# Loading the queries and keys of two attention units together, and moving the second unit's scores ahead of the first unit's PV

## The chip, the cores and the metric

The kernel runs on one core of a Trainium2 chip. The time is in device microseconds (us), measured around the whole execution on the chip. Before the change, 8 runs gave a median of 291.63 us, from 290.91 to 292.34. One further look at the kernel is an execution that was recorded by the hardware profiler.

## What is computed

The inputs q, k and v have the shape 8 x 8 x 576 x 64 (batch, heads, tokens, head dimension), in float32. Attention runs in chunks of 64 tokens; each chunk attends to itself alone. The result goes through two matrix products with a gated activation between them. The reference, cut to its core:

```
q_c = q.reshape(B, H, nc, 64, D)              # the same for k and v; nc = 9
scores = q_c @ k_c.transpose / sqrt(D)
attn = exp(scores - max); attn = attn / sum(attn)
x = (attn @ v_c)  ->  [B*S, H*D]              # 4608 tokens x 512
h = x @ w_in                                  # 512 x 2048
g = h * (1 / (1 + exp(-beta * h)))            # beta has one value per column of h
out = g @ w_out                               # 2048 x 512, float32 result
```

The kernel works in float16 with float32 accumulation. It leaves out the maximum in the softmax (the scores are small) and writes the gate as h * (tanh(beta * h / 2) + 1) / 2.

## The kernel before

**Units and blocks.** The 4608 tokens are cut into 18 units of 256 tokens for the attention, and two units make a block of 512 tokens for the two products. For each unit the kernel goes through these steps:

1. Load q, k (`load_qk`, L102) and two tiles of v (`load_v`, L110) from the GpSimd queue (POOL), converting to float16 on the way. For units 0 to 7, a partition holds two neighbouring tokens.
2. Transpose q and k in blocks of 32x32 on the vector engine (DVE), in `emit_T` (L154).
3. Multiply the scores on TensorE (PE), `emit_sc` (L231), into a PSUM tile of two banks with the tag "s", and take Exp on the scalar engine (ACT), L240.
4. Multiply by v, `emit_pv` (L256), once for each of the two 128-token tiles of the unit, the first into a PSUM tile "x", the second into "s". A column of ones in v gives the sum of the row.
5. Divide by that sum on DVE, `emit_norm`: a reciprocal (L267) and one or two multiplications (L271).
6. Transpose the result, on PE for the first units (`emit_xt_pe`, L287, into PSUM, followed by ACT's copy to the tile xt, L288), later by a DMA.

For each block, `emit_m` makes one 128-row slice m of h (four matmuls, L303, into a PSUM tile "p"), tanh on ACT (L313) and the multiply-add on DVE (L317) into gt; there are 16 slices. `emit_t` makes the second product for one tile of 128 tokens (L335), and ACT copies it out (L345).

**PSUM.** The pool "p" has four buffers of one bank, which are given out in turn; "s" and "x" have one buffer of two banks each. [...]

**The order of the work** is written out by hand: each engine executes its instructions in the order of the calls. The start of the kernel is special:

- Unit 0 is loaded in two halves of four heads. The first half of q and k comes through the queue of the sync engine (SP) as float32 into `raw0`, and is converted on ACT (L173) and DVE (L176). The second half comes through POOL with the conversion (L360). `emit_T_half` transposes a half (L177), `emit_sc_half` multiplies it (L194) and takes Exp (L202). Only after that do PV, norm and the transposes of unit 0 follow.
- Unit 1 is loaded whole by `load_qk(1)`, and its scores come after unit 0 has been transposed.
- The first six slices of block 0 are made in halves: columns 0:256 (unit 0) first, columns 256:512 (unit 1) when unit 1 is done.
- `emit_idle` (L352) multiplies zeros into an unused "p" buffer between these steps. It holds a place in the PE order and keeps the array working.

The order of POOL's loads at the start is: second half of unit 0's q and k; v tiles 0 and 1; q and k of unit 1; w_in group 0; v tiles 2 and 3; the identity for the transposes; w_in groups 1 to 7; w_out groups 0 to 2; unit 2; w_out group 3; unit 3 and later units. Each w_in group holds two slices m.

Of the kernel before, what the change touches and what calls it, by code (L numbers as in the profile page):

```python
# [15 lines left out]
def kernel(  # L16
# [41 lines left out]
    raw0 = [const.tile([128, HH, 2, D], FP32, name=f"raw{i}") for i in range(2)]  # L58
    qk0 = [[const.tile([128, HH, 2, D], FP16, name=f"h0{i}{a}") for i in range(2)] for a in range(2)]
    qkT0 = [[const.tile([128, HH, CH, 2], FP16, name=f"t0{i}{a}") for i in range(2)] for a in range(2)]  # L60
# [81 lines left out]
    def emit_T(u, which=("kT", "qT")):  # L142
# [17 lines left out]
        if "qT" in which and u not in (6, 7, 8):  # L160
            loads_to(u + 4)
# [9 lines left out]
    def emit_T_half(a):  # L171
        if a == 0:
            nc.scalar.copy(out=qk0[a][0], in_=raw0[0])  # L173
        for i in (0, 1):
            if a == 0 and i == 1:
# [3 lines left out]
                    "p (h i r) -> p h r i", h=HH, r=2),  # L179
                in_=qk0[a][i].rearrange("p h r d -> p (h r d)").bitcast(FP32).rearrange(  # L180
                    "p (h r i) -> p h r i", h=HH, r=2),
            )

    def emit_sc_half(a):
        if a == 0:
            et_t[0] = et_p.tile([128, 2, H, CH], FP16, tag="et", name="et")
            x_t["s0"] = ps_s.tile([128, 2, H, CH], FP32, tag="s", name="sc")
        sc = x_t["s0"]
        qt, kt = qkT0[a]
        for h in range(HH):  # L190
            for e in range(2):
                for c in range(4):
                    p0, o0 = 32 * c, 64 * (c % 2)
                    nc.tensor.matmul(  # L194
                        out=sc[o0:o0 + 64, c // 2, HH * a + h, :],
                        lhsT=kt[p0:p0 + 32, h, :, e],
                        rhs=qt[p0:p0 + 32, h, :, e],
                        start=(e == 0),
                        stop=(e == 1),
                    )  # L200
        hs = slice(HH * a, HH * a + HH)
        nc.scalar.activation(out=et_t[0][:, :, hs], in_=sc[:, :, hs], func=ACTF.Exp, scale=scale)  # L202
# [44 lines left out]
    def emit_pv(u):  # L247
        et = et_t.pop(u)
        for s in range(2):
            i = 2 * u + s  # L250
            pool, tag = ((ps_x, "x"), (ps_s, "s"))[s]
            x = pool.tile([128, 2, 4, 128], FP32, tag=tag, name="x")
            for g in range(4):
                for r in range(2):
                    for c in range(2):
                        nc.tensor.matmul(  # L256
                            out=x[64 * c:64 * c + 64, r, g, 0:D + 1],
# [6 lines left out]
    def emit_norm(u, s):  # L264
        x = x_t.pop((u, s))
        rd = rd_p.tile([128, 2, 4, 1], FP32, tag="rd", name="rd")
        nc.vector.reciprocal(out=rd, in_=x[:, :, :, D:D + 1])  # L267
        x16 = x_p.tile([128, 2, 4, D], FP16, tag="x16", name="x16")
        for r in ([0, 1] if u < 2 else [slice(0, 2)]):
            o = x16[:, r]  # L270
            nc.vector.tensor_tensor(  # L271
                out=o, in0=x[:, r, :, 0:D], in1=rd[:, r].to_broadcast(list(o.shape)), op=ALU.mult
            )
# [8 lines left out]
    def emit_xt_pe(u, s):  # L282
        xf = x16_t.pop((u, s)).rearrange("p r h d -> p (r h d)")
        pool, tag = (ps_x, "x") if s == 0 else (ps_s, "s") if u == 2 else (ps_p, "p")
# [69 lines left out]
    with tc.manual_schedule():  # L354
# [3 lines left out]
        for a, eng, dst in ((0, nc.sync, raw0), (1, nc.gpsimd, qk0[1])):  # L358
            for i, src in enumerate((q, k)):
                eng.dma_start(  # L360
                    out=dst[i],
                    in_=src[0, HH * a:HH * a + HH, 0:UNIT, :].rearrange("h (p r) d -> p h r d", r=2),
# [4 lines left out]
        load_v(0)  # L367
        load_v(1)
        load_qk(1)
        load_w_in(0)  # L370
        load_v(2)
        load_v(3)
        nxt[0] = 2
        make_identity(nc, ident)
        for g in range(1, 8):
            load_w_in(g)
# [6 lines left out]
        emit_idle(10, 512)  # L383
        emit_idle(4, 128)
        emit_T_half(0)
        emit_sc_half(0)
        emit_idle(14, 128)
        emit_T_half(1)
        emit_sc_half(1)
        nc.vector.transpose(out=bt, in_=braw)  # L390
        nc.scalar.activation(out=beta2, in_=bt[:, 0:KFF], func=ACTF.Copy, scale=0.5)
        loads_to(4)
        emit_idle(8, 128)
        emit_pv(0)
        emit_norm(0, 0)
        emit_norm(0, 1)
        emit_idle(10, 128)
        emit_xt_pe(0, 0)
        emit_idle(8, 128)
        emit_xt_pe(0, 1)  # L400
        emit_idle(24, 128)
        emit_T(1)
        emit_sc(1, True)
# [4 lines left out]
        emit_pv(1)  # L408
        emit_norm(1, 0)
        emit_norm(1, 1)  # L410
        emit_idle(8, 128)
        v0()
        v1()
        emit_xt_pe(1, 0)
        a0, v0 = emit_m(0, 2, 0, 256, True)
        a1, v1 = emit_m(0, 3, 0, 256, True)
        a0()
        emit_xt_pe(1, 1)
        a1()
        v0()  # L420
        v1()
        emit_m(0, 4, 0, 256)
        emit_m(0, 5, 0, 256)
        for m in range(6):
            emit_m(0, m, 256, 256)
# [166 lines left out]
```

The softmax here doesn't subtract the row's maximum and nothing guards it: scores larger than these inputs give would overflow.

## Time and profile before

| quantity | value |
|---|---|
| median of 8 runs | 291.63 us (290.91 to 292.34) |
| profiled execution: its time / its span | 291.1 us / 289.3 us |
| busy PE, ACT, DVE, POOL | 282.2, 146.3, 139.6, 97.4 us |
| idle matmuls (L352) | 86, busy 9.4 us |
| first product L303: 616 matmuls, second product L335: 560 matmuls | 136.7 us, 131.1 us busy |
| data read from HBM / written | 36.71 MB / 9.44 MB |
| software DMA queue (POOL's loads) | 101216 packets, 18.10 MB as written |

The page gives for each engine the busy time inside the span, which goes from the first to the last instruction. "Busy" of PE overlaps between pipelined matmuls, so a high share doesn't say that the array does useful work: the idle matmuls count too. The chain that ended last says what released each step of the end, and the timeline shows the instructions of a stretch with the idle time ahead of them in brackets and what ended it. A DMA that is issued at one time lands some us later; the trace has the moment at which each of its 16 completions arrived.

### The profile page before, as it was taken

The numbers are of one execution on the slowest core, as the hardware profiler recorded it, in microseconds if no ns is written. First come the engines' busy times: TensorE is split into PE (matmuls) and PEld (weight loads), VectorE is DVE, ScalarE is ACT, GpSimd is POOL, SyncE is SP. The second block draws the span as 40 slices with busy tenths as digits, with TensorE's granted clock in tenths as the row PEclk, the third lists the DMA queues.
The fourth block names the chain that finished last, engine by engine and source line by source line (L and its number), as shares of the span: only waits on it lengthen the run. The fifth ranks groups of instructions, "written<-read, shape, count | busy, mean of one in ns | idle before, by whom it ended". The sixth has DMA issues, their size and how long they took to land.

```text
span 289.3 us, 6592 instructions
## 1 busy us (share of the span) xinstructions
PE 282.2 (98%) x2750; PEld 138.2 (48%) x2750; DVE 139.6 (48%) x254; ACT 146.3 (51%) x227; POOL 97.4 (34%) x126
## 2 busy tenths in 40 slices
PE   7899998999999999999999999999999999999995
PEld 3774455545544444444444444444444444444444
DVE  3477344687267544544453445445453636333300
ACT  3387228773566645454545454455445544444411
POOL 8864578489062994070907060000000000000000
PEclk9999999999999999999999999999999999999999
DMA  9999999999979999999999999524343212001011
GB/s 138 173 196 205 177 179 207 209 167 170 142 82 159 175 186 140 195 119 159 152 155 138 151 136 156 123 61 104 80 109 76 73 37 74 36 36 39 36 73 73
DMA packets 141932, 36.86 MB, mean 127 GB/s; under 512 B 130000, under 2 KB 137424, under 8 KB 141904
## 3 DMA queue, kind: packets, MB, share of 16 engines
q0 software_dynamic: 101216, 18.10, 85.6%
q1 hardware_dynamic: 40544, 18.24, 30.8%
q8 instruction: 21, 0.34, 0.5%
q10 hardware_dynamic: 144, 0.13, 0.1%
q14 instruction: 7, 0.06, 0.1%
HBM read 36.71 MB, written 9.44 MB: 159 GB/s over the span
## 4 chain that ended last, share of the span: by engine, by line
PE 91%; DMA 3%; POOL 2%; DVE 1%; ACT 1%; issue 1%; DVEq 0%; POOLq 0%
PE hps L303 43%; PE ops L335 41%; DMA vbig<-in_v_dram 3%; PE x L256 2%; PE sc L231 1%; PE sc L218 1%; PE ops L547 1%; POOL vbig L110 1%; POOL h L360 1%; ACT xt L288 1%; PE xp L287 1%; DVE x L271 0%; ACT osb L345 0%; ACT sg L313 0%; POOL qu L102 0%
## 5 line engine op out<-in xcount | busy, mean ns | idle before, releaser
L317 DVE SCALAR_TENSOR_TENSOR gt<-sg,hps 128x512 f16<-128x512 f32 (+1 forms) x154 | 99.3, 651 | 114.0 <-ACT sg L313 113.7
L313 ACT ACTIVATE sg<-hps,beta 128x512 f32<-128x512 f32 (+1 forms) x154 | 100.6, 660 | 73.5 <-PE hps L303 73.5
L303 PE MATMUL hps<-xt,win 128*128 128x512 f16 (+1 forms) x616 | 136.7, 366 | 0.3 <-ACT xt L288 0.3
L335 PE MATMUL ops<-wout,gt 128*128 128x512 f16 x560 | 131.1, 379 | 0.0
L303 PEld LDWEIGHTS <-win 128*128 128x128 f16 x616 | 58.2, 98 | 61.3 <-issue 1.0
L335 PEld LDWEIGHTS <-gt 128*128 128x128 f16 x560 | 53.8, 98 | 63.3
L345 ACT ACTIVATE osb<-ops 128x512 f32<-128x512 f32 x35 | 20.9, 598 | 44.4 <-PE ops L335 44.4
L110 POOL DMA_DIRECT2D vbig<-in_v_dram x40 | 34.1, 874 | 10.2 <-DMA wout<-in_moe_w_out_dram 4.3
L96 POOL DMA_DIRECT2D qu<-in_q_dram x22 | 18.8, 865 | 38.9 <-DMA qT<-qu 36.7
L271 DVE TENSOR_TENSOR x<-x,rd 128x512 f16<-128x512 f32 (+1 forms) x40 | 25.1, 637 | 1.4
L96 POOL DMA_DIRECT2D ku<-in_k_dram x22 | 18.8, 882 | 0.0
L240 ACT ACTIVATE et<-sc 128x512 f16<-128x512 f32 (+1 forms) x10 | 7.5, 768 | 9.5 <-PE sc L231 9.5
L267 DVE RECIPROCAL rd<-x 128x8 f32<-128x8 f32 x36 | 7.2, 199 | 9.0 <-PE x L256 9.0
L352 PE MATMUL warm<-idle 128*128 128x128 f16 (+1 forms) x86 | 9.4, 264 | 1.2 <-DVE braw L356 1.2
L224 ACT ACTIVATE et<-sc 128x1024 f16<-128x1024 f32 x10 | 10.2, 1016 | 0.0
L256 PEld LDWEIGHTS <-et 64*64 64x64 f16 x576 | 6.2, 107 | 7.3 <-issue 3.0
L288 ACT COPY xt<-xp 128x512 f16<-128x512 f16 x12 | 6.7, 588 | 4.4 <-PE xp L287 4.4
L102 POOL DMA_DIRECT2D qu<-in_q_dram x10 | 7.8, 785 | 2.8 <-DMA win<-in_moe_w_in_dram 1.6
L256 PE MATMUL x<-vbig,et 64*64 64x65 f16 x576 | 8.4, 195 | 0.2 <-DMA vbig<-in_v_dram 0.2
L102 POOL DMA_DIRECT2D ku<-in_k_dram x10 | 7.7, 770 | 2.3 <-DMA win<-in_moe_w_in_dram 1.3
L154 DVE STREAM_TRANSPOSE kT<-ku 128x512 f32<-128x512 f32 x7 | 5.0, 712 | 5.5 <-DMA ku<-in_k_dram 5.5
L352 PEld LDWEIGHTS <-idle 128*128 128x128 f16 x86 | 5.7, 103 | 4.0 <-issue 2.5
(34 smaller groups left out, 57.0 us busy)
## 6 DMA issues: line engine op xcount, KB each, us to landing
out_dram<-osb SPq DMA_DIRECT2D x35, 256.0 KB, 3.5
vbig<-in_v_dram POOLq DMA_DIRECT2D x32, 128.0 KB, 7.5
qu<-in_q_dram POOLq DMA_DIRECT2D x20, 128.0 KB, 6.1
ku<-in_k_dram POOLq DMA_DIRECT2D x20, 128.0 KB, 6.9
win<-in_moe_w_in_dram POOLq DMA_DIRECT2D x8, 256.0 KB, 9.0
wout<-in_moe_w_out_dram POOLq DMA_DIRECT2D x4, 512.0 KB, 12.5
qu<-in_q_dram POOLq DMA_DIRECT2D x4, 256.0 KB, 6.4
ku<-in_k_dram POOLq DMA_DIRECT2D x4, 256.0 KB, 7.0
```

Of the source, the lines that this page charges most:

```text
L96: nc.gpsimd.dma_start(out=tv[off:off + n, sp], in_=src[b, :, s:s + n, :].rearrange("h p d -> p h d"),)
L102: nc.gpsimd.dma_start(out=t[off // 2:(off + n) // 2], in_=src[b, :, s:s + n, :].rearrange("h (p r) d -> p h r d", r=2),)
L110: nc.gpsimd.dma_start(out=vbig[off:off + n, i, :, 0:D], in_=v[b, :, s:s + n, :].rearrange("h p d -> p h d"),)
L224: nc.scalar.activation(out=et, in_=sc, func=ACTF.Exp, scale=scale)
L256: nc.tensor.matmul(out=x[64 * c:64 * c + 64, r, g, 0:D + 1], lhsT=(et[64 * r:64 * r + 64, s, 4 * c + g, :] if u < XU else et[64 * r:64 * r ...
L271: nc.vector.tensor_tensor(out=o, in0=x[:, r, :, 0:D], in1=rd[:, r].to_broadcast(list(o.shape)), op=ALU.mult)
L303: nc.tensor.matmul(out=hps[:, 0:n], lhsT=w_in16[m // 2][:, kk, (m % 2) * 128:(m % 2) * 128 + 128], rhs=xr[:, c0 // CH:(c0 + n) // CH, 2 * ...
L313: nc.scalar.activation(out=sg[:, 0:n], in_=hps[:, 0:n], func=ACTF.Tanh, scale=beta2[:, m:m + 1])
L317: nc.vector.scalar_tensor_tensor(out=gt_t[j][:, m, c0:c0 + n], in0=sg[:, 0:n], scalar=1.0, in1=hps[:, 0:n], op0=ALU.add, op1=ALU.mult,)
L335: nc.tensor.matmul(out=ops, lhsT=gt_t[j][:, kk, t * 128:(t + 1) * 128], rhs=w_out16[kk // 4][:, kk % 4, :], start=(kk == 0), stop=(kk == K ...
L345: nc.scalar.activation(out=osb, in_=ops, func=ACTF.Copy, scale=0.5)
L352: nc.tensor.matmul(out=d[:, 0:w], lhsT=idle[:, 0:128], rhs=idle[:, 0:w])
```

## The change

- The two halves of q and k at the start hold 512 tokens (units 0 and 1) instead of 256; a partition holds four neighbouring tokens instead of two, so a contiguous piece is 1 KB instead of 512 B. Unit 1's separate load of q and k goes away, and so does its `emit_T(1)` and `emit_sc(1)`.
- `emit_sc_half` takes the unit. Unit 0 lies in partitions 0 to 63 and unit 1 in 64 to 127 of the transposed tiles; the order of the matmuls goes over two row groups instead of four. Unit 1's scores go into a tile "x", and stand ahead of unit 0's PV.
- v tiles 0 to 3 are loaded next, and all w_in groups after these and after the identity.
- PV of tile 1 of each of the two units goes into two "p" buffers instead of "s"; `emit_norm` follows that with a reciprocal and a multiplication for each. For a tile in one buffer it makes a single multiplication, in the first two units too.
- The first four slices of block 0 instead of six are made in halves.
- Idle matmuls are 18 + 5 + 2 + 3 of 512 columns instead of 10 of 512 and 76 of 128.
- `loads_to(5)` is called in one step before PV of unit 0, instead of `loads_to(4)` there and unit 5 with `emit_T(1)`.

```diff
--- before.py
+++ after.py
@@ -55,9 +55,9 @@
     ident = const.tile([128, 128], FP16)
     idle = const.tile([128, 512], FP16)
     HH = H // 2
-    raw0 = [const.tile([128, HH, 2, D], FP32, name=f"raw{i}") for i in range(2)]
-    qk0 = [[const.tile([128, HH, 2, D], FP16, name=f"h0{i}{a}") for i in range(2)] for a in range(2)]
-    qkT0 = [[const.tile([128, HH, CH, 2], FP16, name=f"t0{i}{a}") for i in range(2)] for a in range(2)]
+    raw0 = [const.tile([128, HH, 4, D], FP32, name=f"raw{i}") for i in range(2)]
+    qk0 = [[const.tile([128, HH, 4, D], FP16, name=f"h0{i}{a}") for i in range(2)] for a in range(2)]
+    qkT0 = [[const.tile([128, HH, 128, 2], FP16, name=f"t0{i}{a}") for i in range(2)] for a in range(2)]
     braw = const.tile([128, 32], FP32)
     gate = const.tile([128, 1], FP16)
     bt = const.tile([128, 32], FP32)
@@ -157,7 +157,7 @@
                 in_=a.rearrange("p h r d -> p (h r d)").bitcast(FP32).rearrange(
                     "p (h r i) -> p h r i", h=H, r=2),
             )
-        if "qT" in which and u not in (6, 7, 8):
+        if which[-1] == "qT" and u not in (6, 7, 8):
             loads_to(u + 4)
 
     def emit_gate(u):
@@ -176,30 +176,32 @@
                 nc.vector.tensor_copy(out=qk0[a][1], in_=raw0[1])
             nc.vector.transpose(
                 out=qkT0[a][i].rearrange("p h s e -> p (h s e)").bitcast(FP32).rearrange(
-                    "p (h i r) -> p h r i", h=HH, r=2),
+                    "p (h i r) -> p h r i", h=HH, r=4),
                 in_=qk0[a][i].rearrange("p h r d -> p (h r d)").bitcast(FP32).rearrange(
-                    "p (h r i) -> p h r i", h=HH, r=2),
-            )
-
-    def emit_sc_half(a):
+                    "p (h r i) -> p h r i", h=HH, r=4),
+            )
+
+    def emit_sc_half(u, a):
         if a == 0:
-            et_t[0] = et_p.tile([128, 2, H, CH], FP16, tag="et", name="et")
-            x_t["s0"] = ps_s.tile([128, 2, H, CH], FP32, tag="s", name="sc")
-        sc = x_t["s0"]
+            et_t[u] = et_p.tile([128, 2, H, CH], FP16, tag="et", name="et")
+            pool, tag = ((ps_s, "s"), (ps_x, "x"))[u]
+            x_t["sc", u] = pool.tile([128, 2, H, CH], FP32, tag=tag, name="sc")
+        sc = x_t["sc", u]
         qt, kt = qkT0[a]
         for h in range(HH):
             for e in range(2):
-                for c in range(4):
-                    p0, o0 = 32 * c, 64 * (c % 2)
-                    nc.tensor.matmul(
-                        out=sc[o0:o0 + 64, c // 2, HH * a + h, :],
-                        lhsT=kt[p0:p0 + 32, h, :, e],
-                        rhs=qt[p0:p0 + 32, h, :, e],
-                        start=(e == 0),
-                        stop=(e == 1),
-                    )
+                for s in range(2):
+                    p0 = 64 * u + 32 * s
+                    for c in range(2):
+                        nc.tensor.matmul(
+                            out=sc[64 * c:64 * c + 64, s, HH * a + h, :],
+                            lhsT=kt[p0:p0 + 32, h, 64 * c:64 * c + 64, e],
+                            rhs=qt[p0:p0 + 32, h, 64 * c:64 * c + 64, e],
+                            start=(e == 0),
+                            stop=(e == 1),
+                        )
         hs = slice(HH * a, HH * a + HH)
-        nc.scalar.activation(out=et_t[0][:, :, hs], in_=sc[:, :, hs], func=ACTF.Exp, scale=scale)
+        nc.scalar.activation(out=et_t[u][:, :, hs], in_=sc[:, :, hs], func=ACTF.Exp, scale=scale)
 
     ex_t = {}
 
@@ -244,17 +246,21 @@
         while ex_t[u] and not later:
             emit_ex(u)
 
-    def emit_pv(u):
+    def emit_pv(u, where=("x", "s")):
         et = et_t.pop(u)
         for s in range(2):
             i = 2 * u + s
-            pool, tag = ((ps_x, "x"), (ps_s, "s"))[s]
-            x = pool.tile([128, 2, 4, 128], FP32, tag=tag, name="x")
+            if where[s] == "p":
+                x = [ps_p.tile([128, 4, 128], FP32, tag="p", name=f"y{r}") for r in range(2)]
+            else:
+                pool = {"x": ps_x, "s": ps_s}[where[s]]
+                x = [pool.tile([128, 2, 4, 128], FP32, tag=where[s], name="x")]
             for g in range(4):
                 for r in range(2):
                     for c in range(2):
                         nc.tensor.matmul(
-                            out=x[64 * c:64 * c + 64, r, g, 0:D + 1],
+                            out=(x[0][64 * c:64 * c + 64, r, g, 0:D + 1] if len(x) == 1 else
+                                 x[r][64 * c:64 * c + 64, g, 0:D + 1]),
                             lhsT=(et[64 * r:64 * r + 64, s, 4 * c + g, :] if u < XU else
                                   et[64 * r:64 * r + 64, g % 2, 4 * s + 2 * c + g // 2, :]),
                             rhs=vbig[64 * r:64 * r + 64, i, 4 * c + g, 0:D + 1],
@@ -264,12 +270,12 @@
     def emit_norm(u, s):
         x = x_t.pop((u, s))
         rd = rd_p.tile([128, 2, 4, 1], FP32, tag="rd", name="rd")
-        nc.vector.reciprocal(out=rd, in_=x[:, :, :, D:D + 1])
         x16 = x_p.tile([128, 2, 4, D], FP16, tag="x16", name="x16")
-        for r in ([0, 1] if u < 2 else [slice(0, 2)]):
+        for r, z in [(slice(0, 2), x[0])] if len(x) == 1 else list(enumerate(x)):
+            nc.vector.reciprocal(out=rd[:, r], in_=z[..., D:D + 1])
             o = x16[:, r]
             nc.vector.tensor_tensor(
-                out=o, in0=x[:, r, :, 0:D], in1=rd[:, r].to_broadcast(list(o.shape)), op=ALU.mult
+                out=o, in0=z[..., 0:D], in1=rd[:, r].to_broadcast(list(o.shape)), op=ALU.mult
             )
         x16_t[u, s] = x16
 
@@ -281,7 +287,8 @@
 
     def emit_xt_pe(u, s):
         xf = x16_t.pop((u, s)).rearrange("p r h d -> p (r h d)")
-        pool, tag = (ps_x, "x") if s == 0 else (ps_s, "s") if u == 2 else (ps_p, "p")
+        tag = {(0, 0): "s", (2, 1): "s"}.get((u, s), "px"[s == 0])
+        pool = {"x": ps_x, "s": ps_s, "p": ps_p}[tag]
         xp = pool.tile([128, 4, 128], FP16, tag=tag, name="xp")
         for g in range(4):
             nc.tensor.transpose(out=xp[:, g, :], in_=xf[:, g * 128:(g + 1) * 128], identity=ident)
@@ -359,20 +366,16 @@
             for i, src in enumerate((q, k)):
                 eng.dma_start(
                     out=dst[i],
-                    in_=src[0, HH * a:HH * a + HH, 0:UNIT, :].rearrange("h (p r) d -> p h r d", r=2),
+                    in_=src[0, HH * a:HH * a + HH, 0:2 * UNIT, :].rearrange("h (p r) d -> p h r d", r=4),
                 )
         bv = moe_beta.rearrange("(m w f) -> w m f", w=4, f=32)
         for w in range(4):
             nc.sync.dma_start(out=braw[32 * w:32 * w + KFF, :], in_=bv[w])
-        load_v(0)
-        load_v(1)
-        load_qk(1)
-        load_w_in(0)
-        load_v(2)
-        load_v(3)
+        for i in range(4):
+            load_v(i)
         nxt[0] = 2
         make_identity(nc, ident)
-        for g in range(1, 8):
+        for g in range(8):
             load_w_in(g)
         for g in range(3):
             load_w_out(g)
@@ -380,50 +383,42 @@
         load_w_out(3)
         loads_to(3)
 
-        emit_idle(10, 512)
-        emit_idle(4, 128)
+        emit_idle(18, 512)
         emit_T_half(0)
-        emit_sc_half(0)
-        emit_idle(14, 128)
+        emit_sc_half(0, 0)
+        emit_idle(5, 512)
         emit_T_half(1)
-        emit_sc_half(1)
+        emit_sc_half(0, 1)
+        emit_sc_half(1, 0)
+        emit_sc_half(1, 1)
         nc.vector.transpose(out=bt, in_=braw)
         nc.scalar.activation(out=beta2, in_=bt[:, 0:KFF], func=ACTF.Copy, scale=0.5)
-        loads_to(4)
-        emit_idle(8, 128)
-        emit_pv(0)
+        loads_to(5)
+        emit_idle(2, 512)
+        emit_pv(0, ("s", "p"))
         emit_norm(0, 0)
         emit_norm(0, 1)
-        emit_idle(10, 128)
+        emit_idle(3, 512)
         emit_xt_pe(0, 0)
-        emit_idle(8, 128)
+        emit_pv(1, ("x", "p"))
+        emit_norm(1, 0)
+        emit_norm(1, 1)
         emit_xt_pe(0, 1)
-        emit_idle(24, 128)
-        emit_T(1)
-        emit_sc(1, True)
         a0, v0 = emit_m(0, 0, 0, 256, True)
         a1, v1 = emit_m(0, 1, 0, 256, True)
         a0()
         a1()
-        emit_pv(1)
-        emit_norm(1, 0)
-        emit_norm(1, 1)
-        emit_idle(8, 128)
+        emit_xt_pe(1, 0)
         v0()
         v1()
-        emit_xt_pe(1, 0)
         a0, v0 = emit_m(0, 2, 0, 256, True)
-        a1, v1 = emit_m(0, 3, 0, 256, True)
         a0()
         emit_xt_pe(1, 1)
-        a1()
         v0()
-        v1()
-        emit_m(0, 4, 0, 256)
-        emit_m(0, 5, 0, 256)
-        for m in range(6):
+        emit_m(0, 3, 0, 256)
+        for m in range(4):
             emit_m(0, m, 256, 256)
-        for m in range(6, KFF):
+        for m in range(4, KFF):
             emit_m(0, m)
         emit_T(2)
         for i in range(16):
```

## The prediction

> **What bounds the kernel now.** I read the page first: the shares by engine and the chain that ended last.
>
> ```profile
> span 289.3 us, 6592 instructions
> PE 91%; DMA 3%; POOL 2%; DVE 1%; ACT 1%; issue 1%; DVEq 0%; POOLq 0%
> ```
>
> TensorE ends the run; the rest of the chain is nearly all at the start. So second the chain in order of time, its first 31 us:
>
> ```profile
> 8.04 7.25 DMA vbig<-in_v_dram
> 15.29 0.14 issue
> 15.43 0.32 PE x L256 x16
> 15.75 0.57 PE warm L352 x8
> ...
> 16.75 1.01 PE hps L303 x8
> 17.76 0.22 PE xp L287 x4
> ...
> 18.02 12.44 PE hps L303 x72
> 30.46 6.91 PE ops L335 x32
> ```
>
> Until 15.29 the chain is POOL issuing loads and then the landing of the second unit's last v tile. From 18.02 TensorE never waits for long. Whatever the change wins, it wins by bringing that moment forward. Third, the timeline there:
>
> ```profile
> 4.71 0.38 DVE L176 CAST h<-raw 128x512 f16<-128x512 f32 x1
> 13.00 1.02 PE L231 MATMUL sc<-qT,kT 32*64 32x64 f16 x64 [0.54 <-DVE qT L154]
> 15.43 0.32 PE L256 MATMUL x<-vbig,et 64*64 64x65 f16 x16 [0.18 <-DMA vbig<-in_v_dram]
> 18.02 0.58 ACT L288 COPY xt<-xp 128x512 f16<-128x512 f16 x1 [0.19 <-PE xp L287]
> 35.73 0.71 DVE L154 STREAM_TRANSPOSE kT<-ku 128x512 f32<-128x512 f32 x1 [3.82 <-DMA ku<-in_k_dram]
> 37.30 0.60 PEld L231 LDWEIGHTS <-kT 32*64 32x64 f16 x64 [0.42 <-DVE qT L154]
> ```
>
> Unit 1's scores stand at 13.00, its PV waits for v, and at 37.30 unit 2's scores are held by their k. Loads fill the engines: from 6 us on the DMA share is above 1.4 in each 2 us. The trace's landings: raw q 3.67, raw k 4.54; POOL's q and k half 6.11 and 6.82, v0 7.72, v1 8.55, unit 1's q and k 9.99 and 11.62, first w_in 13.78, v2 14.45, v3 15.29, second w_in 16.67, then 1.33 apart; unit 2's last k 35.63.
>
> [...] before, SP's were done at 3.7 just as POOL's began, so sharing isn't shown. [...] in DMA packets per us, 680 of 512 B read (q, k as 256 B written), 1120 of 256 B (v), 394 of 1 KB (w_in): 348, 287 and 403 GB/s read. [...] here the wide idle matmuls come 0.43 us apart until 5.0. [...] The new score order puts two matmuls on one row group in turn; the PV, which does the same, takes 0.38 us for 32 against 0.32 for scores. I take 0.36.
>
> **The change, part by part.** I follow the start to X, the moment at which the second half (columns 256:512) of block 0's first product begins. From there the new kernel has 4 x 0.432 + 12 x 0.863 = 12.09 us of hps (0.2158 us per 512-wide matmul, from 0.863 for four). Before had the same 12.09 left at 18.02 and reached the ops matmuls at 30.30 by the timeline.
>
> *First loads.* SP: 2 x 512 packets of 1 KB instead of 512 B. Data start near 2.3. Alone until POOL's begin at 3.6, at w_in's 400 GB/s, they move 0.53 MB of 1.05; the other 0.52 at half rate take 2.6 us: 6.2, and 0.75 to the completion (raw q before: last data near 2.9, landing 3.67) gives raw k at **6.75**; bounds 5.5 (SP favoured) and 8.0 (POOL favoured). Raw q lands at 4.2. POOL's q and k half: 1.05 MB, half moved by 6.2, the rest at 400 GB/s, plus 1.2 for the slowest engine (first to last completion of each of these before): q 7.2, k **8.7**. Then v at 0.86 each: 9.6, 10.4, 11.3, **12.1**; w_in 0 13.4 to **14.2** (a 16 KB instruction fetch on one engine cost its predecessor 0.8), w_in 1 15.5. Removed is unit 1's separate q and k; in all, 4096 packets at 680 per us become 2048 at 394: 6.0 us to 5.2. With the slow first microseconds of POOL now filled by SP, the whole stream is about 1 us earlier.
>
> *The queues that these pass.* On SP the four small beta loads stand behind raw k: they land near 8 instead of 5.5 to 7.0, DVE transposes them at 9.5 and the first tanh wants them at 15.2: 5 us of cover. On POOL a load is issued once the eighth before it has landed (the first w_out at 15.58, after v3's 15.29; the seventh w_in at 14.06, after the first's 13.78). Now the third w_in waits for half 1's q, 7.2, the fourth for its k, 8.7, the fifth for v0, 9.6: each issued 2 us or more before the engines reach it at one w_in per 1.33. The identity, now ahead of all w_in, costs POOL 0.6 us near 6.4, with v tiles still queued; cost 0.
>
> *Cast and transposes.* ACT's cast of q, twice the width: 0.62 + 0.42 (the step from 0.60 to 1.02 of Exp, 512 to 1024) = 1.04, done at 5.3, transposed by 6.0, hidden under raw k. DVE's cast of k: between 0.38 and 0.77; 0.66 taken. Transposes of 128x512 stand 0.63 apart in L154. Raw k 6.75 + 0.03 + 0.66 + 0.65 + 0.05 = 8.15: scores (0, half 0), 0.36. The 18 wide idle matmuls (9 at 0.427, 9 at 0.216) end at 6.9 and cost nothing unless the 1.2 us gap cools the array. Then 5 idle x 0.216 = 1.08 to 9.6; DVE has half 1's k at 8.75 + 0.65 + 0.05 = 9.45, just hidden. Scores (0,1), (1,0), (1,1): 3 x 0.36, 2 idle 0.43: PV(0) at **11.1**; its Exp ends at 10.7.
>
> *DVE.* From PV start to reciprocal 0.37. Norms: 0.85 (128x512, from unit 2's rows) for (0,0) and (1,0); for (0,1) and (1,1), each in two PSUM tiles, two pairs 0.22 + 0.335 = 1.11. Starts 11.48, 12.33, 13.44, 14.29; ends 15.45. What waits behind raw k on DVE is half 1's pair of transposes, and behind norm (1,1) the first three products of block 0, which free p buffers for the fourth product and later; both are in the sums.
>
> *PE and PSUM.* PV(1)'s last tile takes the fourth buffer of the p pool, free when norm (0,1) has read it at 12.9; v3 at 12.1 is there. The transposes of (0,1) end near 13.7, ACT's copy starts at 13.9 (0.4 after DVE's last multiply, as at 10.78 and 11.15 before) and takes 0.58 (the L288 group) to 14.5: product 0 starts at **14.5**, product 1 at 15.0 (its buffer is one of norm (1,1)'s, first half read 14.9), product 2 at 15.6 (w_in 1 just there).
>
> *ACT, the last link.* An hps start to its tanh takes 0.65; tanh stand 0.38 apart, a copy 0.49. Tanh 0 15.2, tanh 1 15.6, copy (1,0) 16.0, tanh 2 16.5, copy (1,1) 16.9 to 17.4: X = **17.5**. If tanh take their whole 0.48 the queue gives 17.85. The chain is raw k + 10.75.
>
> *Sum.* 17.5 + 12.09 + 0.1 = 29.7 against 30.3: 0.6 us won; with ACT's dearer spacing 0.25. I take **0.5**. The 58 idle matmuls fewer, 9.4 us busy before, give nothing of themselves: they stood in gaps. Later loads: the POOL order after w_in is unchanged; unit 5's call comes earlier but has the same place in the queue, and its q, k buffers no longer wait for unit 1. Cover that must hold: unit 2's k lands at 35.63 and its transposes free PE at 37.30, exactly as PE arrives at 37.37. PE 0.5 earlier needs that landing 0.43 earlier; the stream gives about 1. If it gives none, the gain is 0.07.
>
> The profiled run took 291.1, 1.8 outside its span and 0.5 under the median 291.63. From the median: 291.63 - 0.5 = **291.1**.
>
> **Rivals.** *Gain absorbed, 291.6*: w_in 0 after 14.9 or unit 2's k not earlier. For: 18.02 was reached with PE waiting only 0.2 for w_in, and 37.30 is tight. Against: fewer packets, and 7.34 MB up to the last w_in must only come 0.5 earlier. *Slower, 292.4*: the first transfers. Scores now start on a raw k twice as large, [...]. Every us after 6.75 moves X one for one (DVE's four norms and ACT's five operations follow it without slack); at 7.25 the gain of 0.5 is gone, at 7.8 the kernel is slower by over 0.58, at 8.0 it stands at 292.4 by the 0.75 gone past zero. For: SP's two first transfers, 0.52 MB together, took from 2.3 to 4.5 with nearly nobody beside them; against: their rate was 330 GB/s with packets of 512 B, and 1 KB reads go at 400. *More, 290.6*: SP favoured, k at 5.5; then POOL's k half at 8.4 decides and, DVE being quicker too, X is 17.1; unit 2's k caps the gain near 1.0. *Cold array, 293*: if the gap at 6.9 to 8.15 lowers the clock, [...] That the scores don't move is excluded: their inputs come in the first four transfers.
>
> **How the numbers follow.** A measurement of this kernel tells about 0.2%, 0.58 us, from no change. Forecast case (gain 0 to 1.0): 0.52, split 0.26 faster and 0.26 within. Absorbed: 0.15, 0.12 within and 0.03 slower. Slower: 0.20; cold 0.03. More: 0.10. Faster 0.36, same 0.38, slower 0.26. The range must reach both sides: 290.3 (gain 1.3) to 292.6 (loss 1.0); the forecast case alone spans 290.6 to 291.6.
>
> **What would show it.** Right: raw k near 6.75, first scores near 8.15, PV(0) at 11.1, product 0 at 14.5 behind ACT's copy and not behind w_in, the second half at 17.5, ops at 29.7, unit 2's k near 34.7 with no longer wait of PE for qT at 37. Wrong: raw k after 7.3; product 0 waiting for w_in; gaps after X; matmuls of 256 columns twice as long after 8 us.

## The result

The changed kernel is slower: a median of 294.69 us (293.41 to 295.88, 11 runs) against 291.65 us (290.77 to 293.55, 32 runs), a ratio of 1.0099 with a 95% interval from 1.008 to 1.0119. The forecast was 291.1 with a range up to 292.6.

The profiled execution took 295.88 us, 294.1 in its span. It is the longest of the recorded runs, so its numbers show the whole of what can go wrong. Page of the changed kernel: span, granted TensorE clock in 40 slices, the queue that carries instructions (packets, MB, share of the DMA engines):

```profile
span 294.1 us, 6449 instructions
PEclk9958999999999999999999999999999999999999
q8 instruction: 21, 0.34, 0.5%
```

The third and fourth slices of the clock (14.7 to 29.4 us) stand at 5 and 8 tenths; before, all stood at 9. The chain in order of time (start, length, what):

```profile
2.13 7.35 DMA h<-in_k_dram
...
10.64 0.49 PE sc L196 x33
...
11.15 1.09 ACT et L204 x2
...
12.28 0.45 PE sc L196 x32
...
13.27 0.30 PE x L261 x16
...
15.97 0.22 PE y L261 x15
16.19 0.87 issue
17.05 0.26 PE y L261
...
18.53 1.87 PE hps L310 x8
...
22.10 13.32 PE hps L310 x68
```

Read it against the prediction's steps. The second scores stand at 10.64 (foreseen 9.6), since half 1's k landed at 9.47. Between them and unit 1's second half stand ACT's two Exp, 1.09 us together, which hold TensorE for 0.94; that wait was not foreseen. The first PV is at 13.20 (11.1). Then the sixteenth and last matmul of unit 1's PV into a "p" buffer (y in the profile) comes 0.87 us late behind "issue": nothing that the profile shows holds it. Product 0 is at 18.53 (14.5), the second halves at 22.1 (17.5), the ops matmuls at 35.26 by the timeline (29.7; before 30.30). From there on the two kernels run alike: 5.0 us behind at 35, 4.8 at the end.

The eight products at 18.53 took 1.87 us where the eight at 16.75 in the kernel before took 1.01. Busy time by windows shows why (stretch, its length, busy us of PE, PEld, DVE, ACT, POOL with counts, granted clock, DMA share, GB/s):

```profile
13.00:18.00 5.00, 3.99 (x77) 2.30 (x76) 3.80 (x12) 1.18 (x4) 2.56 (x5) 0.53 1.45 197
18.00:23.00 5.00, 4.47 (x26) 3.39 (x26) 1.32 (x4) 2.98 (x7) 2.38 (x4) 0.50 1.43 199
```

The array ran at half clock from 13.3 to 23.6; a stretch like this is called a cold array below. Of 12 runs of this kernel with a recorded clock 4 had a mean clock of 1.00 and a median of 293.52; 8 had 0.981 to 0.994 and a median of 294.79. So about 1.9 us of the loss are there without a cold array, and the cold array adds about 1.3 to a run that has it.

### The profile page after: what moved, and what is told of

Read it like the earlier page. It is cut to its first block, busy times and chain, and to the rows that moved or that the text cites. A ratio compares the mean times of both kernels' runs of the same rounds, so it can differ in the third digit from the quotient of the medians.

```text
span 294.1 us, 6449 instructions
## 1 busy us (share of the span) xinstructions
PE 285.1 (97%) x2684; PEld 137.2 (47%) x2684; DVE 140.9 (48%) x250; ACT 146.8 (50%) x225; POOL 96.1 (33%) x124
## 4 chain that ended last, share of the span: by engine, by line
PE 92%; DMA 2%; ACT 2%; DVE 1%; issue 1%; POOL 0%; DVEq 0%; POOLq 0%
PE hps L310 44%; PE ops L342 40%; DMA h<-in_k_dram 2%; PE x L261 2%; PE sc L233 1%; PE sc L220 1%; PE ops L542 1%; PE xp L294 1%; ACT xt L295 1%; PE warm L359 1%; DVE x L277 0%; ACT osb L352 0%; ACT et L204 0%; ACT sg L320 0%; PE sc L196 0%
## 5 line engine op out<-in xcount | busy, mean ns | idle before, releaser
L310 PE MATMUL hps<-xt,win 128*128 128x512 f16 (+1 forms) x608 | 138.6, 373 | 0.9 <-ACT xt L295 0.9
L96 POOL DMA_DIRECT2D qu<-in_q_dram x22 | 18.7, 861 | 48.2 <-DMA qT<-qu 39.3
L277 DVE TENSOR_TENSOR x<-x,rd 128x512 f16<-128x512 f32 x34 | 23.5, 691 | 1.3
L96 POOL DMA_DIRECT2D ku<-in_k_dram x22 | 18.8, 875 | 0.8 <-DMA ku<-in_k_dram 0.7
L359 PE MATMUL warm<-idle 128*128 128x512 f16 x28 | 10.0, 519 | 1.2 <-DVE braw L363 1.2
L226 ACT ACTIVATE et<-sc 128x1024 f16<-128x1024 f32 x10 | 10.2, 1016 | 0.0
L242 ACT ACTIVATE et<-sc 128x1024 f16<-128x1024 f32 (+1 forms) x8 | 6.4, 811 | 7.2 <-PE sc L233 7.2
L102 POOL DMA_DIRECT2D qu<-in_q_dram x9 | 6.8, 768 | 3.1 <-DMA win<-in_moe_w_in_dram 1.3
L102 POOL DMA_DIRECT2D ku<-in_k_dram x9 | 6.8, 760 | 2.6 <-DMA win<-in_moe_w_in_dram 1.5
L128 POOL DMA_DIRECT2D win<-in_moe_w_in_dram x8 | 6.0, 751 | 0.5
```

Of the source, the lines that this page charges most:

```text
L96: nc.gpsimd.dma_start(out=tv[off:off + n, sp], in_=src[b, :, s:s + n, :].rearrange("h p d -> p h d"),)
L102: nc.gpsimd.dma_start(out=t[off // 2:(off + n) // 2], in_=src[b, :, s:s + n, :].rearrange("h (p r) d -> p h r d", r=2),)
L226: nc.scalar.activation(out=et, in_=sc, func=ACTF.Exp, scale=scale)
L277: nc.vector.tensor_tensor(out=o, in0=z[..., 0:D], in1=rd[:, r].to_broadcast(list(o.shape)), op=ALU.mult)
L310: nc.tensor.matmul(out=hps[:, 0:n], lhsT=w_in16[m // 2][:, kk, (m % 2) * 128:(m % 2) * 128 + 128], rhs=xr[:, c0 // CH:(c0 + n) // CH, 2 * ...
L359: nc.tensor.matmul(out=d[:, 0:w], lhsT=idle[:, 0:128], rhs=idle[:, 0:w])
```

## The experiments

Two theories stood at the start. "Late start": several waits add up on the chain to the first PV. "Cold array": only the clock costs. The pause without a cause was first taken for either a buffer or an instruction fetch. The table gives the medians, and the ratio to the kernel before, which was measured beside each on the same chip. The groups e and g, h, and i stood on three chips, so between groups the ratios compare better than the medians; a ratio need not be the exact quotient of the medians.

| run | median us | ratio (95%) | runs with mean clock under 0.997 |
|---|---|---|---|
| changed kernel | 294.69 | 1.0099 (1.008-1.0119) | 8 of 12 |
| e1_exp_after | 295.59 | 1.0138 (1.0114-1.0161) | 4 of 4 |
| e2_contig_T | 293.79 | 1.0075 (1.0048-1.0102) | 5 of 5 |
| e3_warm | 294.33 | 1.0092 (1.0064-1.0119) | 2 of 4 |
| e4_narrow | 296.99 | 1.018 (1.0141-1.022) | 4 of 4 |
| g1_rows | 293.34 | 1.0046 (1.0027-1.0065) | 8 of 20 |
| g2_rows_exp | 292.87 | 1.0038 (1.0017-1.0058) | 10 of 20 |
| g3_pairs | 295.82 | 1.0128 (1.0103-1.0152) | 16 of 18 |
| g4_before_wide | 291.13 | 0.9977 (0.9965-0.999) | 0 of 20 |
| h1_early_rows | 291.84 | 1.0007 (0.9983-1.003) | 7 of 22 |
| h2_all_three | 291.63 | 0.9999 (0.9978-1.002) | 5 of 22 |
| h3_before_rows | 291.24 | 0.9982 (0.9971-0.9993) | 0 of 22 |
| i1_warm | 291.72 | 0.9996 (0.9981-1.0011) | 0 of 22 |

**A wait removed that paid nothing: e1_exp_after.**

```diff
-        emit_sc_half(1, 0)
-        emit_sc_half(1, 1)
+        emit_sc_half(1, 0, False)    # matmuls alone
+        emit_sc_half(1, 1, False)
+        emit_ex_half(1, 0)           # then the two Exp
+        emit_ex_half(1, 1)
```

> Unit 1's two Exp are called after both halves of its scores, so the second half no longer waits on ACT. Theory 'late start' (several waits in the chain to PV add up; this one is the 0.94 us at 12.28): the first PV moves from 13.2 to about 12.3 and the kernel is 0.9 us quicker than the changed one, near 293.8. Theory 'cold array' (only the lower clock costs; the waits are hidden by what follows): no change beyond 0.3 us, 294.5, and the clock still falls in most runs.

Both theories missed. The first PV did move, from 13.20 to 12.22, and the kernel was no quicker: 295.59, with an interval of the ratio that overlaps that of the changed kernel. PE's timeline in this run:

```profile
12.22 0.32 PE L266 MATMUL x<-vbig,et 64*64 64x65 f16 x16
14.06 0.29 PE L266 MATMUL y<-vbig,et 64*64 64x65 f16 x14
16.91 0.27 PE L266 MATMUL y<-vbig,et 64*64 64x65 f16 x2 [2.56 <-issue]
18.39 1.01 PE L315 MATMUL hps<-xt,win 128*128 128x256 f16 x4 [0.67 <-ACT xt L300]
```

PE reached the end of unit 1's PV 1.8 us earlier and then paused 2.56 us instead of 0.87, to practically the same moment, 16.91 instead of 17.05. Something with a time of its own ends this pause. The array was cold in all four runs, in this profile from 16.5 to 23.3; that the longer idle time did it is likely from the place, not shown by itself.

**The transposes: e2_contig_T.** The scores here pair tokens of different chunks; the work of each engine is that of the changed kernel.

```diff
-                    "p (h i r) -> p h r i", h=HH, r=4),     # where the transposes write
+                    "p (h r i) -> p h r i", h=HH, r=4),
```

> The 32x32 transposes of the first q and k write their result in the order they produce it (r outermost) instead of with a step of four words; the scores then pair tokens of different chunks, so the values are not the reference's, while every engine does the same work. If the step makes them slow, they stand 0.63 us apart as the 128x512 ones of unit 2 did, instead of 0.94, and the first and second scores come 0.6 and 0.35 us earlier, 294.3 or less. If the width of four tokens is not the cause, the spacing stays 0.94 and the time 294.7.

DVE's timeline, first of the changed kernel (three transposes merged in the second line), then of this run (two merged in the second):

```profile
5.69 1.11 DVE L177 STREAM_TRANSPOSE t<-h 128x512 f32<-128x512 f32 x1 [3.29 <-ACT h L173]
7.36 3.23 DVE L177 STREAM_TRANSPOSE t<-h 128x512 f32<-128x512 f32 x3
```

```profile
5.70 0.71 DVE L177 STREAM_TRANSPOSE t<-h 128x512 f32<-128x512 f32 x1 [3.31 <-ACT h L173]
7.19 1.30 DVE L177 STREAM_TRANSPOSE t<-h 128x512 f32<-128x512 f32 x2
```

Same tile, same element count: 1.11 us when it writes with a step of four words, 0.71 when it writes without a gap; the trace has the starts of two in a row 0.94 and 0.64 apart. Raw k landed as before (6.04 for 5.99), and the first scores came at 7.96 instead of 8.50. The kernel stood at 293.79, but not by the transposes alone: in this profile half 1's k landed 0.46 earlier as well (9.01), and the pause ended earlier too (16.28), which the next experiments take up.

**Keeping the array busy: e3_warm.**

```diff
-        emit_idle(5, 512)
+        emit_idle(8, 512)
...
         emit_sc_half(1, 0)
+        emit_idle(4, 512)
         emit_sc_half(1, 1)
...
-        emit_idle(3, 512)
+        emit_idle(4, 512)
```

> Idle matmuls added only where TensorE waits anyway: 8 instead of 5 ahead of the second scores, 4 new ones in the wait between unit 1's two halves, 4 instead of 3 ahead of the first output transpose. 'Cold array': the clock stays at 1.00 in all runs and the time falls to that of the changed kernel's runs with full clock, 293.5, or further. 'Late start': the clock stays up, which gives about 1.1 us, and the rest, 1.9 us over the kernel before, stays: 293.5. Both expect the same here; what it tells is how much the clock is worth. If the added matmuls stand in the way, 295.

Half missed: 2 of 4 runs still cooled, now at 18.65 in the profile, after the pause (15.31 to 16.78) and the wait for product 0. Filled were waits at 9.3, 11.3 and 13.6; the pause, which is longer, stayed empty.

**What the pause is: e4_narrow.**

```diff
-        emit_idle(18, 512)
+        emit_idle(72, 128)
...
-        emit_idle(5, 512)   emit_idle(2, 512)   emit_idle(3, 512)     # three places, on one line here
+        emit_idle(20, 128)  emit_idle(8, 128)   emit_idle(12, 128)
```

> The same idle array time in four times as many matmuls of 128 columns (72, 20, 8, 12). If the single 1.1 us pause of TensorE at its instruction 448 (no wait is written there, and a 16 KB instruction transfer precedes it by about 2 us) is an instruction fetch that comes late, the pause stays at instruction 448, which is now inside the idle matmuls ahead of the first PV at about 12.7, and the PV of unit 1 shows none: time within 0.5 us of the changed kernel. If the pause belongs to the PV (buffers), it stays there at the last PV matmul of unit 1.

The place was foretold, the time was not (2.3 us slower). The chain of this run:

```profile
12.66 0.27 PE warm L359 x3
12.93 2.26 issue
15.19 0.44 PE warm L359 x5
15.63 0.25 PE x L261 x16
```

The pause has moved from the PV, where it could have been a buffer, into idle matmuls that read constants and wait for nobody. Counted in program order (each weight load and each matmul is one), it comes at instruction 445 to 448 in each of the seven kernels of the next table, whatever stands there. The trace has a transfer of 16,384 bytes on the instruction queue ahead of each:

| run | instruction 192 reached | transfer starts | pause ends |
|---|---|---|---|
| changed | 10.9 | 14.60 | 17.05 |
| e1_exp_after | 11.1 | 14.50 | 16.91 |
| e2_contig_T | 10.1 | 13.75 | 16.28 |
| e3_warm | 11.0 | 14.48 | 16.78 |
| e4_narrow | 8.9 | 12.88 | 15.19 |
| g2_rows_exp | 7.3 | 10.07 | 12.36 |
| g4_before_wide | 9.8 | 14.22 | 16.50 |

From the start of the transfer to the end of the pause it is 2.3 to 2.5 us each time. The transfer starts 2.8 to 4.4 us after instruction 192, and the pause ends 5.0 to 6.7 us after it. The page of the changed kernel counts 21 such transfers, 0.34 MB, for 5368 weight loads and matmuls: one of 16,384 bytes for about every 256 of them, 64 bytes for each. That PE waits here for instructions which the transfer brings is the author's reading of these times; the profile names nothing that ends the pause. The next transfer fits the reading: in all fourteen traces it starts 3.0 to 3.9 us after PE has reached instruction 448, at 11.1 us or at 17.1. All these times are from a stretch in which the DMA queues are loaded (in the changed kernel 185 GB/s from 10 to 15 us and 194 from 15 to 20, with a DMA share of 1.78 and 1.45); none is from a stretch with idle ones. Even the kernel before had the pause: its transfer started at 11.38 and instruction 448 came at 13.64, its weight load after 0.22 us of "issue". The change put unit 1's 128 score matmuls (256 instructions) in front of the first PV and replaced 76 narrow idle matmuls by fewer wide ones. So PE reached instruction 192 at 10.9 instead of 7.9, and at 16.19, 5.2 us later, it stood in front of 448 and paused.

**More instructions early: g1_rows and g2_rows_exp.**

```diff
-        emit_idle(18, 512)
+        emit_idle(112, 80)     # g2: with the two Exp after both halves as well
```

> The first 18 idle matmuls of 512 columns become 112 of 80: 188 instructions more for TensorE ahead of the first scores, the time about the same. Theory 'instruction fetch': TensorE may not reach instruction 448 + 256 n sooner than 6.1 us after it has reached instruction 192 + 256 n (10.9 to 17.05 in the changed kernel; 6.0 to 6.2 in the four first experiments). The first such pair now lies at about 6.2 and in unit 1's second scores at 12.3, the next at 12.3 and beyond 18.4, so the pause in unit 1's PV is gone, product 0 begins 1 us earlier, and the clock has less reason to fall: 292.5 to 293.5. Rival 'buffers': the pause before the last PV matmul stays and the time is 294.7.

Right: the pause in unit 1's PV is gone, product 0 at 16.48, the median 293.34. PE passed instruction 192 at 6.0, the transfer started at 9.06, and 448 was reached at 12.2, 3.1 us after that start; in the table the pause ended 2.3 to 2.5 us after the start of its transfer. PE's timeline:

```profile
13.05 0.32 PE L261 MATMUL x<-vbig,et 64*64 64x65 f16 x16
14.89 0.30 PE L261 MATMUL y<-vbig,et 64*64 64x65 f16 x16
16.48 1.03 PE L310 MATMUL hps<-xt,win 128*128 128x256 f16 x8 [0.67 <-ACT xt L295]
```

> As the run with 112 idle matmuls, and unit 1's two Exp after both halves of its scores. Instruction fetch: the wait on ACT, which could not pay in the first such experiment because TensorE paused later at the same 16.9, now pays: first PV near 12.5 to 12.9 instead of 13.2, 0.3 to 0.7 us under the run without it. If it still pays nothing, the path from PV on is set by something else (v, norms).

Only partly: in its profile instruction 448 lay in unit 1's scores, and PE paused there from 10.96 to 12.36. The pause took the place of the wait on ACT. In this run the array was at half clock until 7.2 (4.2 in g1_rows's; in the changed kernel until 6.5, where its idle matmuls of 512 columns start 0.43 us apart, and 0.22 apart after that), and instruction 192 was passed at 7.3 instead of 6.0. Its first PV stood at 13.21, so the profile shows no earlier PV. The median gain is 0.47, and the intervals of the two ratios don't tell it from none; by the runs at full clock alone it is 0.76 (292.39 and 293.15).

**Both waits avoided: h1_early_rows.**

From g2_rows_exp, with its two Exp after both halves:

```diff
-        emit_idle(112, 80)
+        emit_idle(98, 48)
+        emit_idle(12, 256)
```

> The changed kernel with unit 1's two Exp after both halves and with the first idle matmuls as 98 of 48 columns and 12 of 256, so that TensorE passes instruction 192 near 5.5 instead of 7: the next pause can only lie at instruction 448, in unit 1's second scores, until 11.6 instead of 12.36. Instruction fetch together with late start: first PV at 12.2 to 12.5 (13.05 with the rows alone), product 0 at 15.6 to 16.0 (16.48), 0.5 to 0.9 us quicker than the run with 112 idle matmuls: 292.4 to 292.9. If the wait on ACT is of no account, 293.3.

The best of the changed family, better than expected: 291.84, level with the kernel before (1.0007). Instruction 192 was passed at 5.0, the transfer started at 8.08, and the timeline has no pause at instruction 448, which came at 11.1. Scores, first PV, product 0 and the second halves:

```profile
10.42 1.00 PE L196 MATMUL sc<-t,t 32*64 32x64 f16 x96 [0.21 <-DVE bt L402]
11.89 0.32 PE L266 MATMUL x<-vbig,et 64*64 64x65 f16 x16
15.30 1.03 PE L315 MATMUL hps<-xt,win 128*128 128x256 f16 x8 [0.67 <-ACT xt L300]
18.23 1.03 PE L315 MATMUL hps<-xt,win 128*128 128x256 f16 x8 [0.57 <-ACT xt L300]
```

The same edit of the two Exp won nothing with the pause behind it, and is part of 1.5 us won here. The start is then level with the kernel before and not ahead of it: the second halves stand at 18.23 (18.02 before) and the ops matmuls at 30.33 (30.30).

**Smaller pieces: g3_pairs.** From g2_rows_exp: the same 512 tokens as two loads of 256 for each q and k, 512 B pieces, transposes at a step of two words, scores over four row groups. The loads:

```diff
-                eng.dma_start(
-                    out=dst[i],
-                    in_=src[0, HH * a:HH * a + HH, 0:2 * UNIT, :].rearrange("h (p r) d -> p h r d", r=4),
-                )
+                for t in range(2):
+                    eng.dma_start(
+                        out=dst[i][:, :, t],
+                        in_=src[0, HH * a:HH * a + HH, t * UNIT:t * UNIT + UNIT, :].rearrange("h (p r) d -> p h r d", r=2),
+                    )
```

> As the former, with the first 512 tokens in two loads of 256 tokens for each q and k, 512 B pieces, and the transposes at a step of two words. If the step of four words is what makes a 128x512 transpose 0.94 us instead of 0.63, they are 0.63 apart here with the same width; the last of the first four pairs ends 0.35 us sooner after its load, the first scores 0.6. The smaller pieces cost DMA time: half 1's k lands at 9.5 or up to 0.8 later. Net between 0.3 quicker and 0.5 slower than the former.

The transposes were as expected:

```profile
9.71 1.90 DVE L177 STREAM_TRANSPOSE t<-h 128x512 f32<-128x512 f32 x3
```

Three in 1.90 us, 0.62 apart. The loads were not (in the kernel before, packets of 512 B had gone at 348 GB/s of data read and those of 1 KB at 403): raw k landed at 7.68 and 8.87 (5.99 in the changed kernel), half 1's k at 9.74 and 10.36, and the first scores stood at 10.48. At 295.82 its median is 3 us above that of the run it was derived from, outside what was expected. Most of this is the clock: 16 of its 18 runs were cold, and the two at full clock (293.25 and 293.36) are 0.9 over the median of g2's at full clock. So at full clock the later loads seem to cost about 0.9, and the array cools more often with them; whether that comes of the smaller pieces or of the doubled number of loads, this run can't tell.

**The idle matmuls alone: g4_before_wide and h3_before_rows.** The kernel before with idle matmuls of equal time:

```diff
-        emit_idle(10, 512)  emit_idle(4, 128)  emit_idle(14, 128)  emit_idle(8, 128)    # from several places
-        emit_idle(10, 128)  emit_idle(8, 128)  emit_idle(24, 128)  emit_idle(8, 128)
+        emit_idle(11, 512)  emit_idle(4, 512)  emit_idle(2, 512)
+        emit_idle(2, 512)   emit_idle(2, 512)  emit_idle(6, 512)   emit_idle(2, 512)
```

> The kernel before with its idle matmuls made wide, the same array time (11, 4, 2, 2, 2, 6, 2 of 512). Instruction fetch: instruction 192 is now in the first PV at 8.4 and 448 in the second PV near 15, more than 6.1 us apart: no pause, the same time as before within 0.3 us. Rival 'the fewer and wider idle matmuls alone make it slower': 292.5 or more.

Missed on both counts: it is slightly quicker than before, 0.9977 (0.9965 to 0.999), and it does pause, for 0.84 us; instruction 192 came at 9.8 and not at 8.4:

```profile
15.15 0.51 PE L256 MATMUL x<-vbig,et 64*64 64x65 f16 x19
16.50 0.29 PE L256 MATMUL x<-vbig,et 64*64 64x65 f16 x13 [0.84 <-issue]
```

Here the pause is largely covered by the wait for w_in: the products behind it stand at 17.39, and the second w_in landed at 16.82. None of its 20 runs cooled. So fewer and wider idle matmuls are not by themselves what makes the changed kernel slower. Why they are a little quicker isn't settled.

```diff
-        emit_idle(11, 512)
+        emit_idle(98, 48)
...
-        emit_idle(4, 512)
+        emit_idle(16, 128)
```

> The kernel before with wide idle matmuls, of which the first are now 98 of 48 columns and the second 16 of 128: instruction 192 is passed near 5.5, 448 lies among the idle matmuls ahead of unit 1's scores at about 12, 704 near 18.2. Instruction fetch: the pause of 1.05 us inside unit 1's PV (15.45 to 16.50 in the profile of the wide version) is gone, and the kernel gains up to that on the wide version: 290.2 to 291.1. If v's landing at 15.3 sets that PV anyway, no gain: 291.1 to 291.4.

The pause went, as foreseen: unit 1's PV ran without a break from 14.73 to 15.15. The gain did not come, 291.24: products 2 and 3 began at 16.95, just after the second w_in had landed at 16.90. That load set it anyway; the expectation had named a load as the reason for no gain, but v's.

**All three, and the clock: h2_all_three and i1_warm.** h2 adds to h1 the edit of e2, again with scores that pair tokens of different chunks.

> The former with the transposes of the first q and k writing in their own order (the scores then pair tokens of different chunks; the work of every engine is the same). If pause, wait on ACT and slow transposes together are what the prediction missed, product 0 comes near 15.2 and the kernel stands at 291.4 to 292.2, level with the kernel before; what remains over the forecast of 291.1 is half 1's k, 0.3 to 0.7 later than foreseen. If another cause is missing, it stays at 292.5 or more.

291.63, inside the range, and 0.2 us under h1; by the runs at full clock alone there is nothing between them (291.54 and 291.41). In its profile half 1's k landed at 10.08 where h1's had 9.18, which takes away what the transposes win. One profile each can't say whether that is chance, so what the slow transposes cost once the pause is gone stays open.

The second, i1_warm, again from h1_early_rows:

```diff
-        emit_idle(12, 256)
+        emit_idle(8, 512)
...
         emit_xt_pe(0, 1)
+        emit_idle(3, 512, "s")      # into the free s tile
...
         emit_m(0, 3, 0, 256)
+        emit_idle(3, 512, "s")
```

(and 6 and 4 instead of 5 and 3 in the two other places)

> The former version of the changed kernel with early instructions and the two Exp after both halves, and wide idle matmuls added in the waits that are left, where they hold nothing up: 8 of 512 instead of 12 of 256 at first, 6 and 4 instead of 5 and 3, and 3 each ahead of product 0 and ahead of the second halves of the products, written to the free s tile. Of 22 runs of the version without them 8 had a mean clock under 0.997, and these took 292.2 to 296.3 against 290.9 to 292.1 for nearly all others. 'Cold array': these runs go, and the median falls from 291.84 to about 291.3, under the kernel before. If cooling has another cause than the idle waits at the start, it stays at 291.8.

The cold runs went: 0 of 22 under 0.997, where h1 had 7 (not the 8 of the expectation), most of them above 293; the longest here took 293.13. The median did not fall to 291.3: 291.72 against 291.92 of the kernel before beside it, no difference. The runs at full clock were 0.3 us slower than h1's, of which 0.2 is the difference of the kernel before on the two chips; in the profile the first scores stood at 9.01 instead of 8.57, with raw k landing 0.4 later (6.51 and 6.11), and whether the added matmuls cost anything isn't settled.

The versions that beat both kernels are the two of the kernel before with wide idle matmuls, g4_before_wide and h3_before_rows, by 0.2%.

## Why the prediction was wrong

*First loads.* Raw k was better than foreseen, 5.99 for 6.75, and half 1's q and k worse, 8.00 and 9.47 for 7.2 and 8.7. The failing term is the half share from 3.6 on, the author's estimate, which no trace of the kernel before showed. The DMA packets of the changed kernel show no sharing there: from 4.0 to 4.5 us SP's queue moved 188 packets and POOL's not one; POOL's began at 4.9, as SP's were ending (the last at 5.5), and from 5.5 to 7.0 went at 326 packets of 1 KB per us, where 394 had been assumed. POOL's start goes by SP's packets and not by the clock: in all fourteen traces POOL issues its first load at about 1.25, and its first packet comes after 885 to 984 of SP's: at 3.55 to 3.81 us where these are 512 B, at 4.91 to 5.11 where they are 1 KB. So a fixed time of readiness doesn't fit; what holds POOL back isn't shown. In g3_pairs, whose SP queue had twice as many packets, both queues move from 3.6 to 8 us; in the changed kernel both move only after 4.9. So of the two rivals about the first loads, the premise of *more* came (SP favoured, raw k early), but with half 1's k at 9.47 where it had 8.4; *slower* had raw k as its late transfer. (By its own sum that rival loses 0.55 at 7.8, not over 0.58.)

*Transposes.* "Stand 0.63 apart in L154" was taken over to a layout with four tokens per partition without asking what the output's step does. It was 0.94, and a single one took 1.07 to 1.11. From half 1's k to the second scores it was 1.17 us for 0.75; with the step gone, in e2_contig_T, it was 0.79. Together with the landing it makes 10.64 of 9.6.

*Scores (0,1), (1,0), (1,1): 3 x 0.36.* This step failed outright. Unit 1's second half writes the tile that Exp of its first half is still reading, and waited 0.94 us for it:

```profile
12.28 0.45 PE L196 MATMUL sc<-t,t 32*64 32x64 f16 x32 [0.94 <-ACT et L204]
```

In the kernel before the same order of calls hid it, because unit 0's halves were more than 1 us apart (5.63 and 7.35). That makes the PV at 13.20 of 11.1. The dearer price of the new order of matmuls, 0.36, wasn't needed: 32 scores take 0.25 to 0.27 us from the first start to the last in the new order, and 0.26 in the old.

*PV to product 0, 3.4; product 0 to the second halves, 3.0; from there 12.19.* These steps hold wherever the pause and the cold clock are out of the way: 3.43, 2.92 and 12.10 in g1_rows, 3.41, 2.93 and 12.10 in h1_early_rows. Norms, ACT's spacing and the buffers were sized rightly. In the changed kernel they were 5.33 and 3.6, through the pause and the cold array.

*"The 58 idle matmuls fewer give nothing of themselves."* What was not counted is instructions. The sum treated PE's program as free to read: it saw the 16 KB transfer on the instruction queue only as a load on one DMA engine, 0.8 us for its neighbour (w_in 0's sixteenth completion at 13.78, its fifteenth at 12.94), and not beside a pause of PE. In the seven kernels of the table PE stood in front of the place 3.2 to 5.9 us after instruction 192, and paused; in g1_rows and h1_early_rows it reached 448 6.2 and 6.1 us after, without a pause. g1_rows, which only adds instructions early, is 1.35 us quicker than the changed kernel.

*Cold array.* Chance wrong: 3 in 100 against 8 runs of 12. It was the author's estimate for the one gap at 6.9 to 8.15; no trace of the kernel before shows what a gap does to the clock. The six runs with a mean clock of 0.992 to 0.994 are 1.2 us longer than those at full clock, the two with 0.981 are 2.3. By the place of the cold stretches, the gaps that cooled it are those that the missed waits made: in the profiles of the changed kernel and of the e runs they begin at 13.3 to 18.7, behind the wait on Exp or the pause, and i1_warm, with wide matmuls in the waits, has none.

*Later cover.* Unit 2's k landed at 34.83, 0.8 earlier (about 1 foreseen). PE came too late to need it.

Put together: two waits on the path (1.0 by loads and transposes, 0.9 by Exp), then a pause that hides part of what either is worth, then the clock. h1_early_rows takes out the Exp wait and the pause and stands at 291.84; the forecast of 291.1 asked for half 1's k 0.5 earlier and transposes 0.3 shorter as well.

## What to carry to other kernels

Count instructions as well as time. In this kernel TensorE paused where it came from instruction 192 to 448 (128 small matmuls and their weight loads) in 3.2 to 5.9 us while the DMA queues were full, and not where it took 6.1 or 6.2. So look for "issue" time at the same instruction number, and test it by adding instructions far ahead of it, which won 1.35 us here. A wait taken away in front of such a pause can pay nothing (e1_exp_after: 295.59 us for 294.69, with the clock low in 4 of 4 runs), and the same edit can win with the pause gone (it is part of 1.5 us in h1_early_rows). When a tile is cut in halves for overlap, check who still reads it (0.94 us here), and price a transpose by the step of its output (1.11 us for 0.71), not by its size alone.

## What was not expected of the hardware

- A pause of TensorE that no semaphore in the profile explains, 0.84 to 2.56 us, at instruction 445 to 448 of the weight loads and matmuls in seven kernels, 2.3 to 2.5 us after a 16 KB transfer on the instruction queue had started.
- The 32x32 transpose of a 128x512 tile: 0.67 to 0.71 us with an output step of one or two words, 1.07 to 1.11 with four.
- In the changed kernel no packet of POOL's queue for about 3 us (2.0 to 4.9) while SP's queue had 1 KB packets to move, and in all fourteen traces POOL's first packet after 885 to 984 of SP's, of 512 B or of 1 KB.
- With idle gaps of 0.9 to 2.6 us between bursts of small matmuls, the clock was halved for 3.4, 6.8 or 10.2 us (10.2 in the changed kernel, from 13.3; 6.8 in e1_exp_after, from 16.5).
